# Moving three of the eight block transposes of a mixer MLP from TensorE to the DMA, and re-splitting its PSUM banks

## The chip, the cores and the metric

The kernel runs on one core of a Trainium2 chip. The time is the device time of one execution in microseconds (us). Each quoted time is a median of several executions. Five engines matter: TensorE (PE in the profile; PEld is its weight load), VectorE (DVE), ScalarE (ACT), GpSimd (POOL) and SyncE (SP), which only issues DMAs here.

A ratio below is the mean time of one kernel's runs over that of the kernel before in the same rounds on the same chip, so it is not quite the ratio of the medians quoted beside it.

## The reference

```python
# x: [1, 2048, 640], w1, w2: [640, 640], w3: [640, 1728], w4: [1728, 640], all bf16
h  = gelu(layernorm(x) @ w1)
hs = concat(four channel groups of h, shifted by +1, -1, +2, -2 tokens) @ w2
x1 = x + hs
out = x1 + gelu(layernorm(x1) @ w3) @ w4
```

## The kernel before

The 2048 tokens are four blocks of 512, each four tiles of 128. I call the matmuls mm1 (w1) to mm4 (w4). mm1 and mm3 need the normalised activations with channels on the partitions, so each of the eight normalised blocks (four per layer norm) is transposed: 20 TensorE transposes into PSUM and three ScalarE evictions. GELU is a ScalarE square, a VectorE instruction (`v`), a ScalarE sigmoid and a VectorE product. An automatic scheduler fixes the order of instructions on each engine when the program is built; the order of the code is only its starting point. It depends on how many buffers each pool has.

```python
_psT_b, _psmm_b, _psres_b = 2, 4, 2       # PSUM buffers: transposes, mm1/mm3, mm2/mm4
...
def transpose_block(src_tiles, dstT, warm_after_pair=0):   # 20 transposes, 3 evictions
    ...  nc.tensor.transpose(psT[...], src_tiles[tt][...], ident[:, :])
    ...  nc.scalar.copy(out=dstT[:, c:c + cn, :], in_=psT[:, 0:cn, 0:BLK])

def mm1_group(b, kc):                     # five matmuls, GELU, products shifted into hsT
    ...
    for (p0, _ch0, ln, grp) in perm[kc]:  # two pieces where a chunk straddles two groups
        col0 = PAD + b * BLK + shifts[grp]
        nc.vector.tensor_tensor(out=hsT[p0:p0 + ln, kc, col0:col0 + BLK], ...)

def mm2_tile(b, tt):                      # per tile: 640 columns as 512 + 128
    ...  matmuls over hsT and w2, and one with the identity that adds x
    nc.scalar.copy(out=x1t[:, n0:n1], in_=ps2[...])
    ln_stats(x1t[:, :], mvb, tt)          # VectorE

def stage_ln2_t2(b):                      # inverse deviation, normalise on VectorE, transpose
    ...
for b in range(NB):                       # the emitted order
    stage_ln1(b)
    for kc in range(DK):
        mm1_group(b, kc)
for b in range(NB):
    for tt in range(TPB):
        mm2_tile(b, tt)
    stage_ln2_t2(b)
for step in range(2, NB + 2):
    emit_B_step(step)                     # mm3 of block b with mm4 of block b-1 between
stage_mm4(NB - 1)
```

One chunk of w1's columns (`w1c`) is gathered on GpSimd before the first mm1. Weights are loaded from two queues, SyncE (w1, w3) and ScalarE (w2, w4).

## Time and profile before

The median was 218.47 us in four runs.

| what | before |
|---|---|
| span of the profiled run | 217.2 us |
| TensorE / VectorE / ScalarE busy | 90% / 77% / 54% of it |
| VectorE busy from 31 to 112.8 us | 77.29 of 81.80 us |
| TensorE busy from 113 to 140 us | 26.84 of 27 us |

The first two lines of the page, its part 1:

```profile
span 217.2 us, 3301 instructions
PE 196.5 (90%) x1200; PEld 100.3 (46%) x1222; DVE 167.3 (77%) x420; ACT 117.8 (54%) x210; POOL 4.7 (2%) x24
```

The table by windows: start and end of the stretch, its length, then busy us and instruction count of each engine, TensorE's granted clock, the DMA share and GB/s.

```profile
24.00:45.00 21.00, 18.13 (x109) 9.16 (x110) 18.58 (x42) 16.44 (x30) 0.00 (x0) 1.00 0.09 34
45.00:65.00 20.00, 18.49 (x129) 10.13 (x131) 19.77 (x64) 14.43 (x29) 0.00 (x0) 1.00 0.01 2
65.00:80.00 15.00, 13.97 (x96) 7.45 (x97) 14.88 (x45) 10.59 (x22) 0.00 (x0) 1.00 0.00 1
80.00:90.00 10.00, 9.58 (x85) 5.40 (x85) 9.52 (x34) 6.81 (x14) 0.00 (x0) 1.00 0.01 2
90.00:100.00 10.00, 9.79 (x50) 4.48 (x49) 9.34 (x29) 8.24 (x16) 0.00 (x0) 1.00 0.00 0
100.00:113.00 13.00, 11.50 (x76) 5.76 (x75) 10.36 (x19) 10.21 (x19) 0.00 (x0) 1.00 0.01 2
31.00:112.80 81.80, 75.65 (x505) 39.71 (x512) 77.29 (x208) 61.36 (x115) 0.00 (x0) 1.00 0.01 1
```

VectorE (third engine column) is nearly full until 100 us. After 113 us TensorE is. The average share of the whole span, 77% for VectorE, hides this.

VectorE's timeline, the groups from 86 to 112 us that waited (start, length, engine, line, operation; in brackets the idle time ahead and what ended it), and ScalarE's timeline at the longest wait:

```profile
88.40 0.89 DVE L192 BATCH_NORM_STATS2 stats<-x 128x6 f32<-128x320 bf16 x2 [0.25 <-ACT x L338]
90.53 0.89 DVE L192 BATCH_NORM_STATS2 stats<-x 128x6 f32<-128x320 bf16 x2 [0.54 <-ACT x L338]
...
109.80 0.69 DVE L374 TENSOR_TENSOR gT<-g,ps 128x512 bf16<-128x512 bf16 x1 [2.20 <-ACT g L273]
```

```profile
106.83 2.42 ACT L261 COPY xn2T<-psT 128x1024 bf16<-128x1024 bf16 x3
109.12 0.65 ACT L273 ACTIVATE g<-v 128x512 bf16<-128x512 bf16 x1
```

Three evictions of the last block's transposes keep ScalarE busy for 2.42 us. The sigmoid that VectorE needs comes after them, and VectorE sits for 2.20 us.

In the view of waits (waiter, cause: total us, times, longest us), mm2 waits for its two PSUM buffers to be evicted:

```profile
PE ps L326 <- ACT x L338: 2.4, 7, 0.5
```

### The profile page before, as it was taken

What the parts mean: (1) busy time and instruction counts of PE and PEld (TensorE: products, weight loads), DVE (VectorE), ACT (ScalarE), POOL (GpSimd) and SP (SyncE); (2) the same over time, 40 slices, a digit from 0 to 9 for tenths busy, and PEclk for the clock granted to TensorE, in tenths of its full rate; (3) what the DMA queues carried; (4) which work ended last, traced back from release to release, by engine and by line L of the source; (5) the groups of instructions that cost most, each with busy time, mean ns of one, the idle gap of its engine ahead of it and who ended that gap; (6) DMA issues with size and microseconds to landing.
All of it is one profiled execution on the core that took longest, in us unless ns stands there. A gap on an engine that the chain in (4) does not pass through costs nothing.

```text
span 217.2 us, 3301 instructions
## 1 busy us (share of the span) xinstructions
PE 196.5 (90%) x1200; PEld 100.3 (46%) x1222; DVE 167.3 (77%) x420; ACT 117.8 (54%) x210; POOL 4.7 (2%) x24
## 2 busy tenths in 40 slices
PE   0669978999889899998999999999999999999994
PEld 0224444454454545544455455455454545544552
DVE  0899879999999999899779667386865966876321
ACT  0004596868678677586885734864753663464000
POOL 4020000000000000000000000000000000000000
PEclk9996999999999999999999999999999999999999
DMA  6999800000000000000000000000000010001011
GB/s 202 364 343 395 297 3 0 0 0 5 0 2 0 3 0 0 3 0 0 2 3 30 30 30 6 29 30 30 3 30 30 0 35 30 0 30 33 30 48 42
DMA packets 8271, 11.50 MB, mean 53 GB/s; under 512 B 512, under 2 KB 7616, under 8 KB 8256
## 3 DMA queue, kind: packets, MB, share of 16 engines
q1 hardware_dynamic: 4672, 6.96, 9.2%
q10 hardware_dynamic: 3584, 4.34, 5.7%
q8 instruction: 9, 0.15, 0.3%
q14 instruction: 6, 0.05, 0.1%
HBM read 8.68 MB, written 2.62 MB: 52 GB/s over the span
## 4 chain that ended last, share of the span: by engine, by line
PE 56%; DVE 30%; ACT 6%; issue 3%; DMA 3%; ACTq 0%; DVEq 0%
PE ps L391 27%; PE ps L366 21%; DVE stats L192 8%; DVE hsT L307 7%; DVE v L269 6%; DVE xn L236 3%; DMA xb<-in_x_dram 3%; PE warm L182 2%; PE ps L297 2%; DVE gT L374 2%; PE psT L253 2%; ACT sq L267 2%; ACT xn2T L261 2%; PE ps L326 2%; DVE mvb L193 1%
## 5 line engine op out<-in xcount | busy, mean ns | idle before, releaser
L267 ACT ACTIVATE sq<-ps 128x512 bf16<-128x512 f32 x76 | 44.7, 596 | 44.2 <-PE ps L366 39.1
L269 DVE SCALAR_TENSOR_TENSOR v<-sq,ps 128x512 bf16<-128x512 bf16 x76 | 50.9, 681 | 20.7 <-ACT sq L267 20.5
L366 PE MATMUL ps<-xn2T,w_sb 128*128 128x512 bf16 (+1 forms) x272 | 64.9, 379 | 1.7 <-DVE gT L374 1.3
L391 PE MATMUL ps<-w_sb,gT 128*128 128x128 bf16 (+1 forms) x443 | 64.3, 298 | 0.6 <-DVE gT L374 0.3
L391 PEld LDWEIGHTS <-gT 128*128 128x128 bf16 x448 | 35.6, 98 | 31.4 <-issue 1.1
L273 ACT ACTIVATE g<-v 128x512 bf16<-128x512 bf16 x76 | 46.6, 626 | 5.3 <-DVE v L269 5.2
L374 DVE TENSOR_TENSOR gT<-g,ps 128x512 bf16<-128x512 bf16 (+1 forms) x56 | 37.4, 680 | 6.0 <-ACT g L273 5.0
L366 PEld LDWEIGHTS <-w_sb 128*128 128x128 bf16 (+1 forms) x280 | 26.2, 99 | 30.6 <-issue 4.7
L326 PE MATMUL ps<-w_sb,hsT 128*128 128x128 bf16 (+1 forms) x155 | 28.4, 296 | 2.8 <-ACT x L338 2.4
L398 DVE TENSOR_TENSOR ot<-ps,x 128x512 bf16<-128x512 f32 (+1 forms) x32 | 15.5, 489 | 11.4 <-PE ps L391 9.4
L307 DVE TENSOR_TENSOR hsT<-g,ps 128x512 bf16<-128x512 bf16 (+3 forms) x32 | 21.9, 687 | 1.6 <-ACT g L273 1.2
L297 PE MATMUL ps<-xnT,w_sb 128*128 128x512 bf16 x78 | 19.3, 378 | 2.1 <-DVE hsT L307 2.1
L182 PE MATMUL warm<-xb,ident 128*128 128x512 bf16 x41 | 12.9, 473 | 7.3 <-DMA xb<-in_x_dram 7.2
L326 PEld LDWEIGHTS <-hsT 128*128 128x128 bf16 x160 | 13.5, 98 | 12.6 <-issue 4.1
L192 DVE BATCH_NORM_STATS2 stats<-xb 128x6 f32<-128x320 bf16 x32 | 14.3, 464 | 6.2 <-DMA xb<-in_x_dram 6.2
L253 PE MATMUL psT<-ident,xn 128*128 128x128 bf16 x160 | 15.3, 224 | 3.1 <-DVE xn L236 2.2
L338 ACT CAST x<-ps 128x512 bf16<-128x512 f32 (+1 forms) x32 | 12.5, 433 | 9.8 <-PE ps L334 9.8
L253 PEld LDWEIGHTS <-xn 128*128 128x128 bf16 x160 | 11.1, 100 | 11.0 <-DVE xn L236 5.9
L192 DVE BATCH_NORM_STATS2 stats<-x 128x6 f32<-128x320 bf16 x32 | 14.6, 476 | 0.8 <-ACT x L338 0.8
L297 PEld LDWEIGHTS <-w_sb 128*128 128x128 bf16 x80 | 7.7, 97 | 11.0 <-issue 3.3
L261 ACT ACT_TABLE_LOAD x1 | 1.3, 1283 | 19.5 <-issue 19.5
L182 PEld LDWEIGHTS <-ident 128*128 128x128 bf16 x42 | 4.7, 116 | 13.3 <-issue 8.8
(30 smaller groups left out, 79.4 us busy)
## 6 DMA issues: line engine op xcount, KB each, us to landing
out_dram<-ot SPq DMA_DIRECT2D x16, 160.0 KB, 1.8
w_sb<-in_w_dram SPq DMA_DIRECT2D x1, 2160.0 KB, 10.6
w_sb<-in_w_dram ACTq DMA_DIRECT2D x1, 2080.0 KB, 11.8
xb<-in_x_dram ACTq DMA_DIRECT2D x2, 640.0 KB, 8.0
xb<-in_x_dram SPq DMA_DIRECT2D x2, 640.0 KB, 7.1
w_sb<-in_w_dram SPq DMA_DIRECT2D x1, 800.0 KB, 12.8
w_sb<-in_w_dram ACTq DMA_DIRECT2D x2, 160.0 KB, 8.3
w_sb<-in_w_dram ACTq DMA_DIRECT2D x2, 120.0 KB, 7.6
```

The source lines that it names most:

```text
L182: nc.tensor.matmul(wps[:, :], lhsT=ident[:, :], rhs=wsrc[:, 0, 0:BLK], start=True, stop=True)
L192: nc.vector.bn_stats(out=stats[:, g, :], in_=src[:, g * gsz:(g + 1) * gsz])
L253: nc.tensor.transpose(psT[:, ci, tt * P:(tt + 1) * P], src_tiles[tt][:, (c + ci) * P:(c + ci + 1) * P], ident[:, :],)
L267: nc.scalar.activation(out=sq[:M, :N], in_=ps[:M, :N], func=ACT.Square, scale=GELU_SQRT_A)
L269: nc.vector.scalar_tensor_tensor(out=v[:M, :N], in0=sq[:M, :N], scalar=1.0, in1=ps[:M, :N], op0=ALU.add, op1=ALU.mult)
L273: nc.scalar.activation(out=g[:M, :N], in_=v[:M, :N], func=ACT.Sigmoid, scale=GELU_SIG_SCALE)
L297: nc.tensor.matmul(ps[:, :], lhsT=w1l[:, k, :], rhs=xTb[:, k, :], start=(k == 0), stop=(k == DK - 1),)
L307: nc.vector.tensor_tensor(out=hsT[p0:p0 + ln, kc, col0:col0 + BLK], in0=g[p0:p0 + ln, :BLK], in1=ps[p0:p0 + ln, :BLK], op=ALU.mult,)
L326: nc.tensor.matmul(ps2[:, 0:n1 - n0], lhsT=hsT[:, k, col0:col0 + P], rhs=w2_sb[:, k, n0:n1], start=(k == 0), stop=not MM2_PE_RES and (k == ...
L366: nc.tensor.matmul(ps[:M, :], lhsT=w3_sb[:, k, f * P:f * P + M], rhs=xT2b[:, k, :], start=(k == 0), stop=(k == DK - 1),)
L374: nc.vector.tensor_tensor(out=gTb[:M, f, :], in0=g[:M, :BLK], in1=ps[:M, :BLK], op=ALU.mult)
L391: nc.tensor.matmul(ps4[:, 0:n1 - n0], lhsT=gTb[:M, f, tt * P:(tt + 1) * P], rhs=w4_sb[:M, f, n0:n1], start=(f == 0), stop=(f == FK - 1),)
```

## The change

The intent is to take work off TensorE and ScalarE: blocks 1 to 3 of the second layer norm are stored to DRAM and read back by one DMA transpose each. Block 0 stays on TensorE, since I expected mm3 to wait for it otherwise. With fewer transposes left, one PSUM bank moves from them to mm2/mm4. The w1c gather moves to ScalarE. The diff also adds switches that are off (other DMA transposes, shifted writes by DMA, parts of the norm on GpSimd); they are cut here.

```diff
-    _psT_b, _psmm_b, _psres_b = 2, 4, 2
+    _psT_b, _psmm_b, _psres_b = 1, 4, 3
...
-                    nc.gpsimd.tensor_copy(out=w1c[:, :, p0:p0 + ln], in_=w1_sb[:, :, ch0:ch0 + ln])
+                    nc.scalar.copy(out=w1c[:, :, p0:p0 + ln], in_=w1_sb[:, :, ch0:ch0 + ln])
...
+    def transpose_block_dma(xnb, dram_t, b, dstT):
+        rows = dram_t[b * BLK:(b + 1) * BLK, :].rearrange("(t p) d -> p t d", p=P)
+        nc.sync.dma_start(out=rows, in_=xnb[:, :, :])
+        nc.sync.dma_start_transpose(out=dstT[:, :, :], in_=dram_t[b * BLK:(b + 1) * BLK, :])
...
     def stage_ln2_t2(b):
...
+        if T2_DMA and b != 0:
+            xnb = xnblk.tile([P, TPB, D], BF16, tag="xnb", name="xnb")
+            for tt in range(TPB):
+                nc.vector.tensor_scalar(out=xnb[:, tt, :], in0=x1_tiles[b * TPB + tt][:, :], ...)
+            transpose_block_dma(xnb, xn2_dram, b, xT2b)
+        else:
+            xn_blk = [ln_apply(...) for tt in range(TPB)]
+            transpose_block(xn_blk, xT2b)
```

More of the change, by code (lines that the diff above doesn't have):

```diff
@@ L97 @@
     X0_SPLIT = False
+    T2_DMA = True
+    T1_DMA = False
+    SHIFT_DMA = False
     wpool = ctx.enter_context(tc.tile_pool(name="wpool", bufs=1))
@@ L106 @@
     gtp = ctx.enter_context(tc.tile_pool(name="gtp", bufs=2))
+    hblkp = ctx.enter_context(tc.tile_pool(name="hblkp", bufs=3))
     temps = ctx.enter_context(tc.tile_pool(name="temps", bufs=4))
     outp = ctx.enter_context(tc.tile_pool(name="outp", bufs=3))
-    _psT_b, _psmm_b, _psres_b = 2, 4, 2
+    _psT_b, _psmm_b, _psres_b = 1, 4, 3
     psT_pool = ctx.enter_context(tc.tile_pool(name="pstp", bufs=_psT_b, space=bass.MemoryType.PSUM))
@@ L112 @@
     psres = ctx.enter_context(tc.tile_pool(name="psres", bufs=_psres_b, space=bass.MemoryType.PSUM))
+    if T1_DMA or T2_DMA:
+        dram = ctx.enter_context(tc.tile_pool(name="dram", bufs=1, space=bass.MemoryType.DRAM))
+        xnblk = ctx.enter_context(tc.tile_pool(name="xnblk", bufs=2))
+    if T1_DMA:
+        xn1_dram = dram.tile([S, D], BF16, name="xn1_dram")
+    if T2_DMA:
+        xn2_dram = dram.tile([S, D], BF16, name="xn2_dram")
     w1_sb = wpool.tile([P, DK, D], BF16, name="w1_sb")
@@ L127, with load_x @@
     nfull = F // P
-    for b in range(NB):
+    LATE_X = NB
+    def load_x(b):
         if b == 0 and X0_SPLIT:
@@ L135 @@
             eng.dma_start(out=x_blocks[b][:, :, :], in_=xblk[b])
+    for b in range(min(LATE_X, NB)):
+        load_x(b)
     nc.sync.dma_start(out=w1_sb[:, :, :], in_=w1.rearrange("(k p) n -> p k n", p=P))
@@ L147 @@
     PSTE_MIX = False
+    PSTE_MIX0 = False
+    RSTD_POOL = False
     if F % P:
@@ L152 @@
             nc.gpsimd.memset(w4_sb[rem:P, nfull, :], 0.0)
+    for b in range(min(LATE_X, NB), NB):
+        load_x(b)
     w1_lhs = {}
@@ L211, in ln_rstd @@
         t1 = statp.tile([P, TPB], FP32, tag="t1", name="t1")
+        reng = nc.gpsimd if RSTD_POOL else nc.vector
         for (mul, add) in ((KADLEC_MUL, KADLEC_ADD), (-0.5, 1.5)):
-            nc.vector.tensor_tensor(out=t1[:, :], in0=y, in1=y, op=ALU.mult)
-            nc.vector.tensor_tensor(out=t1[:, :], in0=t1[:, :], in1=veps[:, :], op=ALU.mult)
-            nc.vector.tensor_scalar(
+            reng.tensor_tensor(out=t1[:, :], in0=y, in1=y, op=ALU.mult)
+            reng.tensor_tensor(out=t1[:, :], in0=t1[:, :], in1=veps[:, :], op=ALU.mult)
+            reng.tensor_scalar(
                 out=t1[:, :], in0=t1[:, :], scalar1=mul, scalar2=add, op0=ALU.mult, op1=ALU.add
             )
-            nc.vector.tensor_tensor(out=y, in0=y, in1=t1[:, :], op=ALU.mult)
+            reng.tensor_tensor(out=y, in0=y, in1=t1[:, :], op=ALU.mult)
         nmr = statp.tile([P, TPB], FP32, tag="nmr", name="nmr")
-        nc.vector.scalar_tensor_tensor(
-            out=nmr[:, :], in0=mvb[:, :, 0], scalar=-1.0, in1=y, op0=ALU.mult, op1=ALU.mult
-        )
+        if RSTD_POOL:
+            nc.gpsimd.tensor_tensor(out=nmr[:, :], in0=mvb[:, :, 0], in1=y, op=ALU.mult)
+            nc.gpsimd.tensor_scalar(
+                out=nmr[:, :], in0=nmr[:, :], scalar1=-1.0, scalar2=0.0, op0=ALU.mult, op1=ALU.add
+            )
+        else:
+            nc.vector.scalar_tensor_tensor(
+                out=nmr[:, :], in0=mvb[:, :, 0], scalar=-1.0, in1=y, op0=ALU.mult, op1=ALU.mult
+            )
         return y, nmr
@@ L257, in transpose_block @@
                     )
-            if PSTE_MIX and ((c // 2) % 2 == 1):
+            if (PSTE_MIX or (PSTE_MIX0 and warm_after_pair > 0)) and ((c // 2) % 2 == 1):
                 nc.vector.tensor_copy(out=dstT[:, c:c + cn, :], in_=psT[:, 0:cn, 0:BLK])
@@ L286, in stage_ln1 @@
         rstd, nmr = ln_rstd(mvb)
-        xn_blk = [ln_apply(xb[:, tt, :], rstd, nmr, tt) for tt in range(TPB)]
         xTb = xtp.tile([P, DK, BLK], BF16, tag="xT", name="xnT")
-        transpose_block(xn_blk, xTb, warm_after_pair=(WARM2 if b == 0 else 0))
+        if T1_DMA:
+            xnb = xnblk.tile([P, TPB, D], BF16, tag="xnb", name="xnb1")
+            for tt in range(TPB):
+                nc.vector.tensor_scalar(
+                    out=xnb[:, tt, :],
+                    in0=xb[:, tt, :],
+                    scalar1=rstd[:, tt:tt + 1],
+                    scalar2=nmr[:, tt:tt + 1],
+                    op0=ALU.mult,
+                    op1=ALU.add,
+                )
+            transpose_block_dma(xnb, xn1_dram, b, xTb)
+            if b == 0:
+                warm_pe(3 * WARM2)
+        else:
+            xn_blk = [ln_apply(xb[:, tt, :], rstd, nmr, tt) for tt in range(TPB)]
+            transpose_block(xn_blk, xTb, warm_after_pair=(WARM2 if b == 0 else 0))
         xnT_blocks[b] = xTb
@@ L304, in mm1_group @@
         g = gelu_chain(ps, P, BLK)
-        for (p0, _ch0, ln, grp) in perm[kc]:
-            col0 = PAD + b * BLK + shifts[grp]
-            nc.vector.tensor_tensor(
-                out=hsT[p0:p0 + ln, kc, col0:col0 + BLK],
-                in0=g[p0:p0 + ln, :BLK],
-                in1=ps[p0:p0 + ln, :BLK],
-                op=ALU.mult,
-            )
+        if SHIFT_DMA and len(perm[kc]) > 1:
+            hbk = hblkp.tile([P, BLK], BF16, tag="hblk", name="hblk")
+            nc.vector.tensor_tensor(out=hbk[:, :], in0=g[:, :BLK], in1=ps[:, :BLK], op=ALU.mult)
+            for (p0, _ch0, ln, grp) in perm[kc]:
+                col0 = PAD + b * BLK + shifts[grp]
+                nc.gpsimd.dma_start(
+                    out=hsT[p0:p0 + ln, kc, col0:col0 + BLK], in_=hbk[p0:p0 + ln, :]
+                )
+        else:
+            for (p0, _ch0, ln, grp) in perm[kc]:
+                col0 = PAD + b * BLK + shifts[grp]
+                nc.vector.tensor_tensor(
+                    out=hsT[p0:p0 + ln, kc, col0:col0 + BLK],
+                    in0=g[p0:p0 + ln, :BLK],
+                    in1=ps[p0:p0 + ln, :BLK],
+                    op=ALU.mult,
+                )
     def mm2_tile(b, tt):
@@ L347, in stage_ln2_t2 @@
         rstd, nmr = ln_rstd(mvb)
-        xn_blk = [
-            ln_apply(x1_tiles[b * TPB + tt][:, :], rstd, nmr, tt, on_act=LN2_NORM_ON_ACT)
-            for tt in range(TPB)
-        ]
         xT2b = xtp2.tile([P, DK, BLK], BF16, tag="xT2", name="xn2T")
-        transpose_block(xn_blk, xT2b)
+        if T2_DMA and b != 0:
+            xnb = xnblk.tile([P, TPB, D], BF16, tag="xnb", name="xnb")
+            for tt in range(TPB):
+                nc.vector.tensor_scalar(
+                    out=xnb[:, tt, :],
+                    in0=x1_tiles[b * TPB + tt][:, :],
+                    scalar1=rstd[:, tt:tt + 1],
+                    scalar2=nmr[:, tt:tt + 1],
+                    op0=ALU.mult,
+                    op1=ALU.add,
+                )
+            transpose_block_dma(xnb, xn2_dram, b, xT2b)
+        else:
+            xn_blk = [
+                ln_apply(x1_tiles[b * TPB + tt][:, :], rstd, nmr, tt, on_act=LN2_NORM_ON_ACT)
+                for tt in range(TPB)
+            ]
+            transpose_block(xn_blk, xT2b)
         xT2_blocks[b] = xT2b
```

## The prediction

> **What bounds it now.** From 31 to 100 us VectorE: the table by windows shows it busy 18.58 of 21, 19.77 of 20, 14.88 of 15, 9.52 of 10 and 9.34 of 10 us (from 24 us on), and the chain of waits runs through its statistics, GELU and hsT instructions. From 113 to 214 us TensorE: idle under 0.6 us in the timeline; one output tile of the last matmul costs 3.80 us, a group of five 128x512 matmuls 1.08. In between neither is full: TensorE 11.50, VectorE 10.36 of 13 us, because three evictions of transposes (2.42 us on ScalarE at 106.8) hold up the GELU chain; VectorE sits 2.2 us.
>
> **What changes.**
> 1. Blocks 1 to 3 of the second layer norm are transposed through DRAM. TensorE loses 60 of 160 transposes, all after 80 us; ten back to back take 0.58 us, so 3.5 us of TensorE (estimate). ScalarE loses nine evictions, 7.8 us. VectorE keeps every instruction.
> 2. Transposes get one PSUM buffer instead of two: 8 transposes, eviction (1.0 us) and the next 8 serialise.
> 3. Residual and output matmuls get three PSUM buffers instead of two: removes the 0.34 us waits for x evictions (2.4 us in the waits view), and 24 instead of 16 early output matmuls can fill TensorE's holes in the first third-matmul block.
> 4. The w1c copy moves from GpSimd (0.88 us, off the path) to ScalarE, whose table load ends only at 20.8 us and whose evictions feed the first matmul: start delayed about 0.9 us.
> 5. The compiled order changes: the third matmul of block 0, which started at 77.6 us among second matmuls, comes after all of them; two blocks of normalisation move into it.
>
> **On the critical path.** VectorE's work up to about 113 us is the same, so most of TensorE's 3.5 us comes off where VectorE binds. VectorE's idle time from 31 to 113 us is about 4.7 us; I expect about 4 after: the ScalarE hold-up (2.2 us) is gone, but 1 us each at the first-norm transposes of blocks 2 and 3 and at the start of the third matmul is new. With +0.9 at the start this cancels. What remains: TensorE enters its own regime with eight more 128x512 output matmuls done (1.7 us) and 0.5 us fewer small waits.
>
> **DMA.** Block 1 needs a 640 KB store and a transpose; about 25 us lie between its normalisation and its first use, and as much for block 2. [...]
>
> **Time.** 216.2 us, 80% range 212.5 to 220.0. Faster by over 2%: 0.23; within 2%: 0.67; slower: 0.10.
>
> **Signs that it is right.** TensorE transposes fall to 100; first mm1 about 0.9 us later; ScalarE total down about 7 us; no TensorE wait for a DMA in the third matmul; from its second block on TensorE over 98% busy.
>
> **What would make it wrong.** [...] First-norm transposes stalling VectorE over 3 us. Or TensorE mattering more before 113 us than I think, so that 3.5 plus 2.2 us come off (about 212 us).

218.47 us less 1.7 us and 0.5 us is 216.27 us, put down as 216.2 us, with the DMA taken as hidden. That it would be hidden stands among the signs: no TensorE wait for a DMA in the third matmul.

## The result, and the profile after

The changed kernel takes 212.79 us (median of 11 runs, 212.67 to 214.71), against 218.8 us before; the ratio is 0.975 (95% interval 0.9723 to 0.9778). The runs fall in two groups, seven from 212.67 to 212.88 us and four from 214.15 to 214.71 us; I call the first the good group, 212.7 us. Experiment 8 comes back to this. The gain is 6.0 us where 2.3 us was predicted, just inside the stated range. The direction was right and the size was not.

Part 1 of the page after:

```profile
span 210.9 us, 3189 instructions
PE 191.5 (91%) x1140; PEld 96.4 (46%) x1162; DVE 165.5 (78%) x420; ACT 111.6 (53%) x203; POOL 3.7 (2%) x22
```

Its table by windows. The last line runs to the last GELU product of block 0 in mm3, as the line that ends at 112.80 does in the table before; both begin as long after the first mm1.

```profile
24.00:45.00 21.00, 19.25 (x116) 9.49 (x117) 17.69 (x40) 16.16 (x29) 0.00 (x0) 1.00 0.09 32
45.00:65.00 20.00, 18.93 (x124) 10.00 (x126) 19.81 (x51) 16.23 (x32) 0.00 (x0) 1.00 0.00 1
80.00:90.00 10.00, 9.21 (x54) 4.50 (x54) 10.00 (x45) 7.29 (x15) 0.00 (x0) 1.00 0.37 98
90.00:100.00 10.00, 9.16 (x45) 4.28 (x46) 10.00 (x28) 5.36 (x10) 0.00 (x0) 1.00 0.43 132
100.00:113.00 13.00, 12.88 (x67) 5.89 (x67) 12.15 (x21) 10.51 (x19) 0.00 (x0) 1.00 0.34 90
31.75:107.70 75.95, 71.66 (x448) 36.51 (x455) 74.73 (x208) 55.41 (x108) 0.00 (x0) 1.00 0.15 41
```

From the start of that line VectorE does as many instructions (208) in 75.95 us as before in 81.80. Its idle time falls from 81.80 - 77.29 = 4.5 us to 75.95 - 74.73 = 1.2 us, and the busy time itself falls by 2.6 us.

TensorE, ScalarE and VectorE where mm3 begins, from the three timelines:

```profile
83.05 4.48 PE L435 MATMUL ps<-xn2T,w_sb 128*128 128x512 bf16 x20
```

```profile
84.33 0.60 ACT L299 ACTIVATE sq<-ps 128x512 bf16<-128x512 f32 x1 [0.66 <-PE ps L435]
```

```profile
85.08 0.46 DVE L212 BATCH_NORM_STATS2 stats<-x 128x6 f32<-128x320 bf16 x1
85.44 0.16 DVE L234 TENSOR_TENSOR t<-yi 128x4 f32<-128x4 f32 x1
85.50 0.70 DVE L301 SCALAR_TENSOR_TENSOR v<-sq,ps 128x512 bf16<-128x512 bf16 x1
```

mm3 starts at 83.05 us, and the square that its first `v` needs is done at 84.93 us (84.33 + 0.60). VectorE still has statistics to do until 85.50 us. It has a backlog there, by a margin of 0.6 us, so the slow start of mm3's GELU chain costs it nothing.

The waits of mm2 for evictions, and the DMA issues (KB each where known, us from issue to landing):

```profile
PE ps L382 <- ACT x L394: 0.4, 1, 0.4
```

```profile
xn_dram<-xnb SPq DMA_DIRECT2D x3, 640.0 KB, 3.2
...
xn2T<-xn_dram SPq DMA_TRANSPOSE x3, 4.9
```

A block's round trip through DRAM takes 3.2 + 4.9 = 8.1 us, and the view of waits has no TensorE wait for it: block 1's transpose landed at 91.9 us, and mm3 of block 1 starts at 104.7 us. The three transposes of 640 KB took 4.7 to 5.1 us from issue to landing: at the median of 4.9 us, 655,360 bytes are 134 GB/s, and 20 blocks of 128x128 are about 245 ns each. SyncE's queue was held 2.7 to 3.0 us by each transpose, and 0.39 us by the store ahead of the first, which has the same size.

To see where the 6.3 us of span (217.2 to 210.9) come from, I cut each profiled run at two events of VectorE's timeline: the start of the first `v`, and the end of the last GELU product of block 0 in mm3. Between them VectorE is nearly full; after them TensorE is. The two events, before and then after (the end is 112.20 + 0.67 and 107.08 + 0.67 us):

```profile
25.94 0.69 DVE L269 SCALAR_TENSOR_TENSOR v<-sq,ps 128x512 bf16<-128x512 bf16 x1 [0.83 <-ACT sq L267]
112.20 0.67 DVE L374 TENSOR_TENSOR gT<-g,ps 64x512 bf16<-64x512 bf16 x1
```

```profile
26.69 0.69 DVE L301 SCALAR_TENSOR_TENSOR v<-sq,ps 128x512 bf16<-128x512 bf16 x1 [1.68 <-ACT sq L299]
107.08 0.67 DVE L443 TENSOR_TENSOR gT<-g,ps 64x512 bf16<-64x512 bf16 x1
```

| profiled run | first `v` at | to the last product of block 0 | rest of the span | early mm4 matmuls |
|---|---|---|---|---|
| before | 25.9 us | 86.9 | 104.3 | 16 |
| after | 26.7 us | 81.1 | 103.1 | 24 |

The last column is the number of mm4 matmuls that the compiled TensorE order puts ahead of the last mm3 matmul of block 0. So the start lost 0.8 us, VectorE's stage gave 5.9 us, and TensorE's stage gave 1.2 us. The prediction had +0.9, about -0.7 and -2.2 us for these three. The cut means something only because one engine is nearly full in each part: VectorE is busy for 81.2 us of the 86.9 before and for 78.6 of the 81.1 after, TensorE for 100.7 us of the 104.3 and for 99.4 of the 103.1.

### The profile page after: what moved, and what is told of

Its sections match the earlier page's. It is cut to its first block, busy times and chain, and to the rows that moved or that the text cites. A ratio compares the mean times of both kernels' runs of the same rounds, so it can differ in the third digit from the quotient of the medians.

```text
span 210.9 us, 3189 instructions
## 1 busy us (share of the span) xinstructions
PE 191.5 (91%) x1140; PEld 96.4 (46%) x1162; DVE 165.5 (78%) x420; ACT 111.6 (53%) x203; POOL 3.7 (2%) x22
## 4 chain that ended last, share of the span: by engine, by line
PE 56%; DVE 28%; DMA 6%; ACT 3%; ACTq 2%; issue 2%; SPq 0%; DVEq 0%
PE ps L460 28%; PE ps L435 25%; DVE hsT L363 9%; DVE v L301 6%; DMA w_sb<-in_w_dram 6%; DVE stats L212 5%; DVE xn L263 2%; ACTq L168 2%; PE ps L344 2%; DVE xnb L408 1%; DVE gT L443 1%; DVE mvb L213 1%; PE warm L202 1%; ACT L305 1%; ACT L184 1%
## 5 line engine op out<-in xcount | busy, mean ns | idle before, releaser
L435 PE MATMUL ps<-xn2T,w_sb 128*128 128x512 bf16 (+1 forms) x272 | 63.6, 379 | 2.0 <-DVE gT L443 1.4
L460 PE MATMUL ps<-w_sb,gT 128*128 128x512 bf16 (+1 forms) x442 | 63.6, 298 | 0.3
L382 PE MATMUL ps<-w_sb,hsT 128*128 128x512 bf16 (+1 forms) x156 | 27.0, 297 | 0.6 <-ACT x L394 0.4
L344 PE MATMUL ps<-xnT,w_sb 128*128 128x512 bf16 x78 | 19.9, 379 | 1.5 <-DVE hsT L363 1.3
L285 PE MATMUL psT<-ident,xn 128*128 128x128 bf16 x100 | 9.4, 219 | 4.7 <-DVE xn L263 3.1
L285 PEld LDWEIGHTS <-xn 128*128 128x128 bf16 x100 | 7.0, 97 | 10.7 <-DVE xn L263 5.8
L293 ACT COPY xnT<-psT 128x1024 bf16<-128x1024 bf16 (+1 forms) x12 | 10.5, 874 | 2.2 <-PE psT L285 2.1
```

Source lines behind the costliest of these rows:

```text
L285: nc.tensor.transpose(psT[:, ci, tt * P:(tt + 1) * P], src_tiles[tt][:, (c + ci) * P:(c + ci + 1) * P], ident[:, :],)
L344: nc.tensor.matmul(ps[:, :], lhsT=w1l[:, k, :], rhs=xTb[:, k, :], start=(k == 0), stop=(k == DK - 1),)
L382: nc.tensor.matmul(ps2[:, 0:n1 - n0], lhsT=hsT[:, k, col0:col0 + P], rhs=w2_sb[:, k, n0:n1], start=(k == 0), stop=not MM2_PE_RES and (k == ...
L435: nc.tensor.matmul(ps[:M, :], lhsT=w3_sb[:, k, f * P:f * P + M], rhs=xT2b[:, k, :], start=(k == 0), stop=(k == DK - 1),)
L460: nc.tensor.matmul(ps4[:, 0:n1 - n0], lhsT=gTb[:M, f, tt * P:(tt + 1) * P], rhs=w4_sb[:M, f, n0:n1], start=(f == 0), stop=(f == FK - 1),)
```

## The experiments

The theories: A, the removed TensorE and ScalarE work is what counts. B, the PSUM split, with the order and the buffers that it gives, is what counts. The experiments undo one part or do one part alone. Each edit also changes the order that the scheduler compiles, so no run changes a part and nothing else.

### 1. The DMA transposes alone

```diff
 # the changed kernel with
-    _psT_b, _psmm_b, _psres_b = 1, 4, 3
+    _psT_b, _psmm_b, _psres_b = 2, 4, 2
-                    nc.scalar.copy(out=w1c[...], in_=w1_sb[...])
+                    nc.gpsimd.tensor_copy(out=w1c[...], in_=w1_sb[...])
```

> The kernel before with only the DMA transposes of blocks 1 to 3 (two transpose buffers, two residual/output buffers, w1c on GpSimd). Theory A (the removed TensorE and ScalarE work is what counts): 213 us or less, nearly the whole gain of 6 us. Theory B (the PSUM split and the order that follows from it are what counts, the removed work falls where VectorE binds): 216 to 218 us.

Measured: 214.79 us, ratio 0.9791 (0.9758 to 0.9824). That is 2.1% of the 2.5% that the whole change gave, so A holds for most of it, but neither number was met. In its profile VectorE's stage is 81.8 us, 5.1 us shorter than before, while the rest, 105.0 us, is not shorter at all (104.3 before). The waits of mm2 for evictions are still there: `2.4, 7, 0.5`.

### 2. The PSUM split alone

```diff
 # the kernel before with
-    _psT_b, _psmm_b, _psres_b = 2, 4, 2
+    _psT_b, _psmm_b, _psres_b = 1, 4, 3
```

> The kernel before with only the PSUM split 1/4/3, all transposes on TensorE, w1c on GpSimd. Its compiled order already has the third matmul after all second matmuls, as in the changed kernel. Theory A: no gain or a small loss, 218 to 220 us. Theory B: 214 to 215 us.

Measured: 215.89 us, ratio 0.985 (0.9823 to 0.9877). B holds as well: with all 160 transposes on TensorE the split alone is worth 1.5%. VectorE's stage is 82.9 us, 4.0 shorter than before, and the rest 105.0 us, again not shorter. The compiled order has 14 early mm4 matmuls.

### 3. The w1c gather back on GpSimd

```diff
-                    nc.scalar.copy(out=w1c[...], in_=w1_sb[...])
+                    nc.gpsimd.tensor_copy(out=w1c[...], in_=w1_sb[...])
```

> The changed kernel with the w1c copy back on GpSimd. The copies on ScalarE (0.59 and 0.33 us) stand before evictions that feed the first matmul, which starts 0.75 us later than before. If that delay reaches the end: 0.7 us faster than the changed kernel, 212.0 us. If it is absorbed: the same.

Measured: 212.09 us, ratio 0.9678 (0.965 to 0.9706). The span is 0.7 us shorter than that of the changed kernel (210.2 against 210.9 us), and so is the time to the first `v` (26.0 against 26.7 us), while both later stages are the same. So the delay reaches the end. Its size is less sure, since the two profiled runs differ in clock (mean granted clock 1.000 here, 0.992 in the changed kernel), though in both the second group of transposes waited for ScalarE's eviction (0.94 and 0.49 us), not for matmuls at a lower clock. The two runs of this experiment with a clock of 0.989 and 0.992 took 212.43 and 212.24 us, 0.3 to 0.5 us less than the changed kernel's 212.74 us.

This run also combines experiments 1 and 2: they give 2.1% and 1.5%, and both together 3.2%, a little less than the sum. Against experiment 2, which differs from it by the DMA transposes alone, it is 3.8 us faster (212.09 against 215.89); against experiment 1, which differs by the PSUM split alone, 2.7 us.

### 4. TensorE's and ScalarE's work put back, into a scratch tile

```diff
             transpose_block_dma(xnb, xn2_dram, b, xT2b)
+            # for each pair of chunks: 8 transposes of xnb into psT, then
+                scr = temps.tile([P, 2, 512], BF16, tag="scr", name="scr")
+                nc.scalar.copy(out=scr[:, 0:cn, :], in_=psT[:, 0:cn, 0:BLK])
```

> The changed kernel, with DMA transposes kept, and the 60 TensorE transposes and nine evictions done as well, into a scratch tile that nobody reads. Theory A: all of what the DMA saved comes back, 216 us or more. Theory B: at most 2 us slower than the changed kernel, under 215 us.

Measured: 217.24 us, ratio 0.9897 (0.9849 to 0.9944). The runs fall in two groups: 215.88 us once, and 217.23 to 217.54 us three times. The profiled run (217.23 us) has its first `v` at 28.2 us, 1.5 us later than the changed kernel; experiment 8 tells why. The good group is 3.2 us above the changed kernel's good group (212.7 us). That rests on one run; the slower groups of both kernels are 2.9 us apart (217.25 against 214.3 us). It is what the removed work is worth where the PSUM split is already made: more than B's limit of 2 us, and about what A asked for. In the profile VectorE's stage is 83.0 us, 2.0 us longer than in the changed kernel, and the rest is 104.2 us, 1.1 us longer.

### 5. One transpose buffer, two mm2/mm4 buffers

```diff
 # the kernel before with
-    _psT_b, _psmm_b, _psres_b = 2, 4, 2
+    _psT_b, _psmm_b, _psres_b = 1, 4, 2
```

> The kernel before with one transpose buffer and still two residual/output buffers (1/4/2; one bank unused). If the third residual/output buffer made the 3.4 us of the PSUM split: no gain or a loss, 218.5 to 220 us. If the new order or the single buffer made it: 217 us or less.

Measured: 219.2 us, ratio 1.0001 (0.9964 to 1.0038). No gain, though the compiled order changes here as well. mm2's waits stay (`2.3, 7, 0.5`), and the compiled order has 12 early mm4 matmuls. VectorE's stage is 85.1 us, 1.8 us shorter than before, and the rest 106.2 us, 1.9 us longer. In sum, losing a transpose buffer costs nothing; the gain of experiment 2 needs the third mm2/mm4 buffer.

### 6. Only TensorE's transposes put back

This is experiment 4 without the scratch copies.

> The changed kernel with the 60 TensorE transposes done as well, without the nine evictions. [...] If TensorE's time is what counts: +2.5 us or more, 215.2 us or above. If ScalarE's evictions are what counts: under 214 us. [...]

The 2.5 us is to be read against the 3.2 us of experiment 4.

Measured: 215.91 us, ratio 0.9848 (0.98 to 0.9895), again in two groups (215.1 and 216.7 us). The good group is 2.4 us above the changed kernel's, a shade under the 2.5 us expected, and experiment 4's is 0.7 to 0.8 us above that. So of the 3.2 us that the removed work is worth, TensorE's transposes are 2.4 and the evictions 0.8. The profile shows where: VectorE's stage is 81.4 us, only 0.3 us longer than in the changed kernel, and the rest is 105.1 us, 2.0 us longer. Beside experiment 4 this says that the evictions cost 1.6 us in VectorE's stage, and that the rest took part of this back. The compiled order has 10 early mm4 matmuls in place of 24.

### 7. Weight loads off ScalarE's queue

In the profile before, ScalarE evicts nothing until its queue has issued all loads of w2 and w4, the last of which holds it from 15.5 to 19.5 us; its first eviction comes at 20.8 us. These loads move to SyncE, with w1c on GpSimd.

```diff
-            nc.scalar.dma_start(out=w2_sb[...], in_=w2[ch0:ch0 + ln, :])
+            nc.sync.dma_start(out=w2_sb[...], in_=w2[ch0:ch0 + ln, :])
 # the same for the two loads of w4
```

> The changed kernel with w1c on GpSimd and the loads of w2 and w4 issued from SyncE, so that ScalarE's queue no longer waits for loads until 19.5 us. Transposes of the first block end at about 18 us, so the first matmul could start about 2.5 us earlier than 24.1 us, and the end moves by as much if VectorE is the limit from there on: 209.5 us. If VectorE's backlog of statistics fills that time anyway: 211 to 212 us.

Measured: 211.66 us, ratio 0.9653 (0.9602 to 0.9705), in two groups: 210.7 to 210.8 and 212.5 to 212.6 us. The first mm1 comes at 22.9 us, where it was 24.1 us in experiment 3: half of the expected gain. The 2.5 us was wrong because the warm-up matmuls stand between the transposes on TensorE: ScalarE's first eviction comes at 18.3 us, but the second group of transposes starts only at 20.7 us, behind 12 warm-up matmuls begun at 18.1 us and without idle time before it.

### 8. The shifted halves written by DMA as well

```diff
 # the kernel of experiment 7 with
-    SHIFT_DMA = False
+    SHIFT_DMA = True     # one full-width VectorE product, then DMA writes of its pieces into hsT
```

> As the run before it, and the shifted hsT halves of the three straddling chunks are written by DMA after one full-width VectorE instruction: 12 of 32 VectorE instructions of 0.67 us go, 8 us of VectorE's stage. TensorE then limits: I expect 3 to 6 us off the run before it, 204 to 207 us. If the DMA writes land late, TensorE waits on hsT and the gain is gone.

Measured: 210.45 us, ratio 0.9599 (0.9551 to 0.9647), in two groups: 209.6 and 211.2 to 211.3 us. It is correct and the fastest kernel, ahead of the change (0.975). But it missed its expectation of 204 to 207 us. VectorE's stage falls to 78.3 us and TensorE takes over as the limit (65% of the chain that ended last, 56% in the changed kernel): the rest is 104.6 us, with 16 early mm4 matmuls.

The two groups go with TensorE's clock. In experiments 7 and 8 every run of the fast group had a mean granted clock of 0.999 or 1.000, and every run of the slow group 0.990 to 0.992. Windows of TensorE in experiment 8, a run of its slow group, and then in experiment 7, a run of its fast group (busy, clock, DMA share, GB/s):

```profile
18.00:20.00 2.00, 2.00 (x9) 0.50 1.03 419
20.00:21.00 1.00, 1.00 (x4) 0.50 1.01 386
```

```profile
18.00:20.00 2.00, 2.00 (x14) 1.00 1.04 419
20.00:21.00 1.00, 1.00 (x10) 1.00 0.98 386
```

The two programs are the same up to here. With the clock at 0.50, the 12 warm-up matmuls end 1.7 us later, and the first mm1 comes at 24.5 in place of 22.9 us. In experiment 4's profile the half-clock stretch lay later, from 22.4 to 25.8 us (0.50 in the windows from 23 to 25 us), over the transposes ahead of the first mm1. By the same view, each of these stretches near the start was 3.4 us long: 18.1 to 21.5 us in the kernel before, 17.8 to 21.2 us in the changed kernel, 17.9 to 21.3 us in experiment 8.

What decides between the groups is not shown. From 14 to 16 us, ahead of the stretch, TensorE was busy for 0.39 us in experiment 8 and for 1.41 us in experiment 7, where the clock stayed full; from 16 to 18 us it was busy for 0.84 and 0.83 us. No run varied this alone.

In the changed kernel and in experiments 4 and 6 the mean clock, 0.990 to 0.992 in both groups, does not tell them apart. The place of the half-clock stretch may; that this makes their slow groups is not shown. The distance between the groups (1.4 to 1.8 us over the five kernels) is about the 1.7 us above.

### 9. The third mm2/mm4 buffer, with two transpose buffers

```diff
 # the kernel before with
-    _psT_b, _psmm_b, _psres_b = 2, 4, 2
+    _psT_b, _psmm_b, _psres_b = 2, 3, 3
```

> The kernel before with three residual/output buffers and still two transpose buffers; the bank comes from the main matmuls (2/3/3 in place of 2/4/2). Its compiled order, too, has the third matmul after all second ones. If the third residual/output buffer made the gain of the PSUM split: 215 to 217 us, unless the lost main buffer costs more. If the gain needs the single transpose buffer too: 218.5 us or more.

Measured: 216.93 us, ratio 0.9907 (0.9861 to 0.9954). The third buffer alone gives a gain, even at the price of a main buffer, so together with experiment 5 it is what the split needs to pay. The gain is 0.9%, not the 1.5% of experiment 2, and it lies elsewhere: the compiled order has 23 early mm4 matmuls, the rest is 102.9 us and VectorE's stage 86.0 us, where experiment 2 gained in VectorE's stage (82.9 us) and not in the rest (105.0 us).

### 10. Blocks 2 and 3 of the first layer norm by DMA too

```diff
 # the kernel of experiment 8 with
-        if T1_DMA:                 # and T1_DMA = False
+        if T1_DMA and b > 1:       # and T1_DMA = True
```

> The fastest so far (loads on SyncE, shifted halves by DMA; 210.5 us), and blocks 2 and 3 of the first layer norm go through the DMA transpose as well: 40 more TensorE transposes gone (2.3 us by 58 ns each) and six evictions. TensorE limits that kernel from 30 us on, so I expect the time to fall by about 2 us, to 208.3 us. If VectorE limits the stage again, nothing.

Measured: 211.33 us, ratio 0.9622 (0.9556 to 0.9687). No gain, by the intervals not to be told from experiment 8. The clock blurs this comparison: the runs at 0.992 (209.96 and 210.51 us) are faster than experiment 8's at 0.991 and 0.992 (211.23 and 211.28 us), and no run had the full clock. The profiled run is the slowest of the four. In it the round trip has no slack: VectorE's normalisation of block 2 ends at 36.0 us, and TensorE, idle from 43.7 us, gets the transposed block at 46.4 us. TensorE's timeline and the view of waits:

```profile
46.38 2.31 PE L344 MATMUL ps<-xnT,w_sb 128*128 128x512 bf16 x5 [2.71 <-DMA xnT<-xn_dram]
```

```profile
PE ps L344 <- DMA xnT<-xn_dram: 2.7, 1, 2.7
```

TensorE waits 2.7 us for the transposed block. The five matmuls behind the wait take 2.31 us, where 1.24 us is usual, and the next five 1.83 us. The granted clock was 0.91 over 45 to 65 us, and 1.00 from 24 to 45 us and from 65 to 113 us. The wait and the lower clock came together. How much of the gain from the 40 removed transposes they ate was not separated.

## Why the prediction was right or wrong

**Right: the regimes.** VectorE limits up to the last product of mm3's block 0, TensorE after it. VectorE is busy 74.73 of 75.95 us up to there, and TensorE 26.84 of 27 us from 113 to 140 us.

**Right: the start.** "Start delayed about 0.9 us": 0.8 us. Experiment 3 shows that it reaches the end: 0.7 us by the medians, 0.3 to 0.5 us between runs of about the same granted clock.

**Right: the DMA is hidden.** Store plus transpose took 8.1 us, where the prediction saw about 25 us of slack and the profile after shows 21.2 us for block 1, and no TensorE wait for a DMA in mm3.

**Right in kind: the counts.** TensorE has 60 instructions fewer, ScalarE is busy 6.2 us less (117.8 to 111.6), and TensorE is still at 26.84 of 27 us from 113 to 140 us.

**Wrong: "I expect about 4 after".** This is the first of two terms that failed in VectorE's stage, which gave 5.9 us where 0.7 was forecast. VectorE's idle time was to fall from 4.7 to 4 us, since three new stalls of 1 us each were to eat the gain. Before, it was 4.5 us, as estimated; after, it is 1.2 us, a fall of 3.3 us. None of the three stalls exists: no gap of VectorE above 0.23 us stands between 31 and 107 us. I had asked how long the transposes and mm3's first group take, and not whether VectorE would have work queued meanwhile. It had: at the start of mm3 its statistics end 0.6 us after the first square is ready. What the idle time goes with is ScalarE's nine evictions, as the prediction said of the 2.2 us hold-up, and not TensorE's transposes. Counted in the same way (from 6.97 us after the first mm1 to the last product of block 0), VectorE idles 1.1 to 1.2 us in every run without these evictions in which VectorE still writes the shifted halves itself (the changed kernel, experiments 1, 3, 6 and 7), with TensorE's transposes in place in experiment 6 and mm2's waits in place in experiment 1. It idles 2.4 to 4.8 us in every run with the evictions (4.5 before; 2.6, 2.4, 2.9 and 4.8 in experiments 2, 4, 5 and 9). The closest pair is experiments 4 and 6, which differ by the evictions alone and by the order that follows: 2.4 and 1.1 us. The PSUM split alone (experiment 2) had already brought the 4.5 us down to 2.6.

**Wrong: "VectorE's work up to about 113 us is the same".** This is the second term, and nearly as large: the instructions are the same, but VectorE is busy with them for 2.6 us less. More than half of this is in the smallest ones. From the start times in the trace, the 64 tiny instructions of the inverse deviation in this stage occupied VectorE for 6.1 us before and 4.7 us after, as the new order puts them differently between long ones. The mean length of one did not change (155 and 156 ns before and after); they overlap more. No run isolates this, so it is a reading of the two traces, not a tested cause.

**Wrong: "most of TensorE's 3.5 us comes off where VectorE binds", and the 2.2 us of TensorE's own stage.** That stage gave 1.2 us, half of the forecast, although the eight more early mm4 matmuls are there (24 against 16). By experiment 6, putting the transposes back costs 2.4 us of those 3.5, and 2.0 of them appear in the rest, where TensorE binds. My reading is that TensorE time freed in VectorE's stage can be filled with mm4 matmuls, as long as PSUM has a buffer for them; no run fixes the order and frees the time. A longer run of early mm4 matmuls mostly goes with a shorter rest: 23 and 24 with 102.9 and 103.1 us, 16 with 104.3, 104.6 and 104.9, 14 and 15 with 105.0 and 104.2, 10 and 12 with 105.1 and 106.2. Experiment 1 does not fit: 18 with 105.0 us. So the prediction's point 3 named the right mechanism for the third buffer, but by this reading the removed transposes feed the same mechanism, and it did not count them there.

**What stays open.** How the 5.9 us of VectorE's stage divide between the evictions' absence, the order and the buffers is separated only in part: the evictions account for 1.6 us where the split is made (experiments 4 and 6). Both parts alone give most of the 5.9 us (5.1 and 4.0 us), so they overlap there. In the rest each part alone loses 0.7 to 0.8 us, and only both together gain 1.2 us. That the times nearly add up is the sum of these two, and not a sign that the parts are independent.

## What to carry to other kernels

Work taken off an engine that is not the limit in a stage was still worth something here (2.4 us in experiment 6), by the reading above because that engine may run ahead into the next stage; ask what it can do early, and whether a PSUM buffer is free to do it. A new stall of a limiting engine cost nothing here where the engine had a backlog when it came (0.6 us at the start of mm3), so follow its queue, not the latency of what feeds it. A DMA transpose cost no wait where the schedule had slack for its whole round trip (8.1 us of the 21.2 us from block 1's store to its first use), and showed no gain in experiment 10, where the next matmul stood right behind it and waited 2.7 us. When runs of one kernel fall in two groups, compare good group with good group, and look at the granted clock first (0.999 to 1.000 against 0.990 to 0.992 in experiments 7 and 8).
